# Loads of x0 and Wv in one queue on ACT, and half chunks of the output in three 64-row visits

## Chip, cores, metric

One core of a Trainium2 chip. The metric is the device time of one execution in microseconds (us), as the median of the runs in the fast state. "Span" is the length of the profiled execution, some 1.6 to 2.2 us less than the time. Ratios are the mean time of one kernel's fast runs over the mean of the other's fast runs of the same rounds, so not quite the ratio of the medians quoted beside them. The experiments ran on different chips. Kernels are compared only within the same rounds. Landings, waits and starts come from one profiled execution of each kernel.

## The reference, cut to what matters

```python
g = sigmoid((x * gate_w).sum(-1))                     # x: 2048 x 448
qkv = x @ wqkv                                        # 16 heads of 28
pq, pk = q @ w_phi, k @ w_phi                         # per head
phi = concat(softmax(p), softmax(-p))
kv, z = phi_k^T v, sum(phi_k)
a = (phi_q kv / (phi_q z + 1e-6)) @ wo
b = gelu(x @ w1 + b1) @ w2 + b2                       # 448 -> 1792 -> 448
out = g * a + (1 - g) * b
```

The kernel makes b and a in one PSUM tile per 128 rows of x: fourteen matmuls with w2 ("dense"), then those with wo. The quotient phi_q kv / den is made per tile in a "num" block (`nm`, `den`, `o_tok`) and transposed by a DMA into `oT`.

## The kernel before

The start. `gate` and the constants are left out; `...` marks cuts.

```python
nc.scalar.dma_start(x0, x[0:512, :] ...)                       # 448 KB
nc.sync.dma_start(gate[0:1, :], gate_w[None, :])
for c, eng in ((0, nc.sync), (1, nc.scalar), (2, nc.sync)):    # Wv, 112 KB each
    eng.dma_start(WvG[:, c, 0:D], A_wqkv[c * P:(c + 1) * P, 2 * D:3 * D])
nc.scalar.dma_start(WvG[64:P, 3, 0:D], A_wqkv[384:448, 2 * D:3 * D])
nc.scalar.dma_start(wphi[:, 0:3, :], ...)                      # 384 rows of 56 bytes
...
load_wT(WkT, D)            # DMA transposes of the key and query weights, on SP
load_wT(WqT, 0)
load_x(1)                  # DMA transposes of rows of x, on SP
...
dummies(7)                 # PE: keeps the array busy until x0 is there
turn_x0(0, xp[0])          # PE: 8 transposes, then a copy to xT
turn_gate()                # PE: gate's column; ACT casts it into column 448 of each WvG part
turn_x0(1, xp[1])
fill_bd()
v_pair(0, on_act=True)     # PE: V of tiles 0..3, needs all four parts of WvG
v_pair(1)
prep(WkT, ...)             # PE: first weight product (w_ps), needs WkT, then WqT
prep(WqT, ...)
```

The output. Four closing matmuls with wo (the fourth holds 64 rows of wo and b2) for tiles 0 to 3, three and a 64-row one for the others:

```python
for t in range(4):
    dense_out(y[:, 0:D], t, full, True, (6, 7) if t == 2 else ())   # num 6, 7 in its middle
    ...                                                              # num blocks, attn_out(..., NC4)
for g in range(4, NT, 4):
    ...
    y_ends(group[0:2], g)          # two pairs of 64-row matmuls open four tiles
    y_ends(group[2:4], g + 2)
    for t in range(g, g + 4):
        ...                        # dense_out, num blocks, attn_out(..., 3)
```

Ahead of it, while PE works on the 28 hidden units: `if n == 8: nc.sync.dma_start(w2_sb[:], ...)`, 1568 KB. It can't come sooner in one piece, since w2_sb's space holds q tokens until the DMA transposes have read them.

The softmax here doesn't subtract the row's maximum and nothing guards it: scores larger than these inputs give would overflow.

## Time and profile before

| | before |
|---|---|
| time, median (range) of the first three runs | 149.19 us (149.19 to 149.71) |
| span | 147.7 us |
| PE busy | 97% |
| x0 landed | 3.99 us |
| Wv's four parts landed (in the order 0, 1, 2, 3) | 4.88, 4.34, 5.53, 5.30 us |
| first V matmul / first weight product | 5.87 / 9.16 us |
| first num block to the start of the last matmul | 57.70 us |

Landings and starts are read from the trace's records; a landing is the time at which the semaphore of a DMA is full.

### The profile page before, as it was taken

What the parts mean: (1) busy time and instruction counts of PE and PEld (TensorE: products, weight loads), DVE (VectorE), ACT (ScalarE), POOL (GpSimd) and SP (SyncE); (2) the same over time, 40 slices, a digit from 0 to 9 for tenths busy, and PEclk for the clock granted to TensorE, in tenths of its full rate; (3) what the DMA queues carried; (4) which work ended last, traced back from release to release, by engine and by line L of the source; (5) the groups of instructions that cost most, each with busy time, mean ns of one, the idle gap of its engine ahead of it and who ended that gap; (6) DMA issues with size and microseconds to landing.
All of it is one profiled execution on the core that took longest, in us unless ns stands there. A gap on an engine that the chain in (4) does not pass through costs nothing.

```text
span 147.7 us, 3133 instructions
## 1 busy us (share of the span) xinstructions
PE 143.8 (97%) x1302; PEld 75.0 (51%) x1302; DVE 85.0 (58%) x134; ACT 75.3 (51%) x91; POOL 68.7 (47%) x50
## 2 busy tenths in 40 slices
PE   7999999999999999999999999999999999999992
PEld 2674545555544954444444455654555455545561
DVE  3443799999999899999200037760287237611112
ACT  1655999988899337777776760113211201221100
POOL 7999999999977999919940000000000000000000
PEclk9999999999999999999999999999999999999999
DMA  4999999999800099991999913394134103410111
GB/s 147 245 226 176 148 196 221 218 217 217 178 2 2 11 161 146 193 189 26 144 172 172 346 64 71 72 87 123 62 71 107 62 31 89 104 47 31 56 37 31
DMA packets 44962, 18.08 MB, mean 122 GB/s; under 512 B 36754, under 2 KB 44948, under 8 KB 44948
## 3 DMA queue, kind: packets, MB, share of 16 engines
q1 hardware_dynamic: 43732, 17.22, 59.2%
q10 hardware_dynamic: 1152, 0.65, 1.6%
q8 instruction: 10, 0.16, 0.5%
q14 instruction: 4, 0.03, 0.1%
q0 software_dynamic: 64, 0.01, 0.0%
HBM read 6.34 MB, written 1.84 MB: 55 GB/s over the span
## 4 chain that ended last, share of the span: by engine, by line
PE 97%; DVE 0%; issue 0%
PE y L520 29%; PE hp L467 29%; PE pq L348 7%; PE y L532 7%; PE v_ps L332 4%; PE pk L340 4%; PE pk L233 3%; PE nm L480 3%; PE acc L355 3%; PE v_ps L214 2%; PE warm_ps L386 2%; PE v_ps L233 2%; PE w_ps L264 1%; PE xp L369 1%; PE y L526 1%; PE pk L220 1%
## 5 line engine op out<-in xcount | busy, mean ns | idle before, releaser
L520 PE MATMUL y<-w_sb,gel 128*128 128x448 bf16 (+2 forms) x238 | 45.4, 342 | 0.0
L467 PE MATMUL hp<-xT,w_sb 64*128 64x512 bf16 x196 | 42.6, 376 | 0.0
L467 PE MATMUL hp<-xS,w_sb 64*128 64x512 bf16 x196 | 42.6, 376 | 0.0
L472 ACT ACTIVATE gel<-hp,b1T 128x1024 bf16<-128x1024 f32 x28 | 30.8, 1110 | 13.2 <-PE hp L467 13.2
L520 PEld LDWEIGHTS <-gel 128*128 128x128 bf16 x238 | 22.2, 98 | 19.8 <-issue 0.9
L467 PEld LDWEIGHTS <-w_sb 64*128 64x128 bf16 x392 | 18.9, 94 | 23.1
L308 POOL TENSOR_TENSOR phik<-phik,rec 128x1792 bf16<-128x1792 bf16 (+1 forms) x8 | 24.9, 3127 | 1.3 <-DVE rec L305 1.3
L546 ACT ACTIVATE b2u<-b_sb,ungate 128x448 f32<-128x448 bf16 x12 | 7.9, 666 | 28.7 <-DVE res L538 28.7
L484 DVE TENSOR_SCALAR den<-nm,einv 128x16 f32<-128x16 f32 x16 | 3.7, 229 | 29.5 <-PE nm L480 29.4
L538 DVE SCALAR_TENSOR_TENSOR res<-y,ungate,b2u 128x448 bf16<-128x448 f32 (+2 forms) x13 | 8.4, 648 | 17.1 <-PE y L532 17.1
L303 DVE TENSOR_REDUCE sums<-phik 128x64 f32<-128x1792 bf16 x8 | 16.0, 1999 | 3.2 <-ACT phik L294 3.2
L308 POOL TENSOR_TENSOR oT<-oT,rec 128x1792 bf16<-128x1792 bf16 x4 | 12.7, 3213 | 1.1 <-DVE rec L305 1.1
L532 PE MATMUL y<-wo_sb,oT 128*128 128x448 bf16 (+2 forms) x55 | 12.4, 342 | 0.0
L348 PE MATMUL pq<-Wpq,xT 64*128 64x448 bf16 x56 | 11.5, 349 | 0.0
L348 PE MATMUL pq<-WqS,xS 64*128 64x448 bf16 x56 | 11.4, 349 | 0.0
L308 POOL TENSOR_TENSOR w_sb<-w_sb,rec 128x1792 bf16<-128x1792 bf16 x3 | 9.6, 3213 | 3.0 <-DVE rec L305 3.0
L487 DVE TENSOR_TENSOR o_tok<-nm,den 128x448 bf16<-128x448 f32 x16 | 10.0, 624 | 0.6
L305 DVE RECIPROCAL rec<-sums 128x64 f32<-128x64 f32 x16 | 8.8, 553 | 1.9 <-DVE sums L303 0.5
L202 DVE CAST vaug<-v_ps 128x896 bf16<-128x896 f32 x7 | 7.5, 1072 | 3.0 <-PE v_ps L214 2.5
L536 ACT ACTIVATE res<-y,ungate 128x448 bf16<-128x448 f32 x4 | 2.5, 634 | 12.7 <-PE y L532 12.7
L293 ACT ACTIVATE phik<-pk 128x896 bf16<-128x896 f32 x8 | 7.6, 947 | 1.5 <-PE pk L222 1.5
L303 DVE TENSOR_REDUCE sums<-oT 128x64 f32<-128x1792 bf16 x4 | 7.9, 1973 | 0.0
(116 smaller groups left out, 180.6 us busy)
## 6 DMA issues: line engine op xcount, KB each, us to landing
w_sb<-in_B_w_dram SPq DMA_DIRECT2D x4, 784.0 KB, 11.5
out_dram<-res SPq DMA_DIRECT2D x15, 112.0 KB, 1.8
w_sb<-in_B_w_dram SPq DMA_DIRECT2D x1, 1568.0 KB, 7.3
xS<-xT SPq DMA_DIRECT2D x2, 256.0 KB, 4.0
EqT<-in_A_x_dram ACTq DMA_DIRECT2D x1, 448.0 KB, 3.2
xS<-xT SPq DMA_DIRECT2D x2, 192.0 KB, 3.9
wo_sb<-in_A_wo_dram SPq DMA_DIRECT2D x1, 336.0 KB, 16.9
oT<-o_tok SPq DMA_TRANSPOSE x16, 2.4
```

Of the source, the lines that this page charges most:

```text
L293: nc.scalar.activation(out=dst[:, :, :, 0, 0:PW], in_=src, func=ACT.Exp)
L303: nc.vector.reduce_sum(out=sums[:], in_=ph, axis=AX.X)
L305: nc.vector.reciprocal(out=rec[:], in_=sums[:])
L308: eng.tensor_tensor(out=ph[:, lo:hi], in0=ph[:, lo:hi], in1=rec[:, lo:hi, :, None].to_broadcast([P, hi - lo, 2, DH]), op=ALU.mult)
L348: nc.tensor.matmul(pq[:, i, 0:D], lhsT=x_half(i, k, h)[:, r * P:(r + 1) * P], rhs=w_half(Wpq, WqS, i, k), start=(k == 0), stop=(k == NK - 1))
L467: nc.tensor.matmul(hp[:, i, :], lhsT=w1_sb[i * HP:(i + 1) * HP, k, j * P:(j + 1) * P], rhs=x_half(i, k, h), start=(k == 0), stop=(k == NK ...
L472: nc.scalar.activation(out=gel[h][:, j, :], in_=hp[:].rearrange("p a b -> p (a b)"), func=ACT.Gelu_apprx_tanh, bias=b1T[:, j:j + 1])
L487: nc.vector.tensor_tensor(out=o_tok[:, t % 4, 0:D].rearrange("p (x h d) -> p x h d", x=NPR, h=2), in0=nmv[:, :, 0:PW].rearrange("p x (h d) ...
L520: nc.tensor.matmul(y, lhsT=gel[t // 8][:, j, (t % 8) * P:(t % 8 + 1) * P], rhs=w2_sb[:, j, cols], start=(opens and j == 0), stop=False)
L532: nc.tensor.matmul(y, lhsT=oT[:, c, tok], rhs=wo_sb[:, c, cols], start=False, stop=(c == chunks - 1))
L538: nc.vector.scalar_tensor_tensor(out=res[:, cols], in0=y, scalar=ungate[:, t:t + 1], in1=b2u[t][:, cols], op0=ALU.mult, op1=ALU.add)
L546: nc.scalar.activation(out=b2u[t][:], in_=b2_sb[:], func=ACT.Copy, scale=ungate[:, t:t + 1])
```

## The change

Its intent: x0, which PE waits for, gets through first, with all of Wv behind it in one queue, and the small load of w_phi goes to the otherwise idle SP; in the output, tiles 0 to 3 too use 64-row matmuls for their half chunk, and all sixteen are gathered in three visits.

```diff
-    for c, eng in ((0, nc.sync), (1, nc.scalar), (2, nc.sync)):
+    for c, eng in ((0, nc.scalar), (1, nc.scalar), (2, nc.scalar)):
         eng.dma_start(WvG[:, c, 0:D], A_wqkv[c * P:(c + 1) * P, 2 * D:3 * D])
     nc.scalar.dma_start(WvG[64:P, 3, 0:D], A_wqkv[384:448, 2 * D:3 * D])
-    nc.scalar.dma_start(wphi[:, 0:3, :], ...)
+    nc.sync.dma_start(wphi[:, 0:3, :], ...)
 ...
-    nc.sync.dma_start(wo_sb[:, 0:3, :], ...)          # and two small loads more
+    nc.sync.dma_start(wo_sb[:], ...)
 ...
-        if t % 2 and t > 3:
+        if t % 2:
             nc.vector.tensor_copy(out=o_tok[:, t % 4, D:512], in_=o_tok[:, t % 4, D - HP:D])
 ...
+    def visit(closing, opening):                      # 64-row matmuls, then DVE finishes `closing`
+        ...
+    ahead = {0: (2, 3), 1: (4, 5), 2: (6, 7), 3: (8,), 4: (9,), 5: (10, 11),
+             8: (12,), 9: (13,), 10: (14,), 11: (15,)}  # num blocks behind the dense part of a tile
+    ...
+        if t == 3:
+            visit((0, 1, 2, 3), (4, 5))
+        elif t == 7:
+            visit((6, 7), (8, 9, 10, 11))
+        elif t == 13:
+            visit((12, 13), (14, 15))
```

Also dropped: one memset on DVE, one on POOL. Tiles 0 to 3 are now finished by DVE instead of ACT.

More of the change, by code (lines that the diff above doesn't have):

```diff
@@ L77 @@
     w2_sb = consts.tile([P, NJ, D], BF16, name="w2_sb")
-    wo_sb = consts.tile([P, NC4, D], BF16, name="wo_sb")
+    wo_sb = consts.tile([P, 3, D], BF16, name="wo_sb")
     EqT = consts.tile([P, NPR, S], BF16, name="EqT")
@@ L127 @@
     nc.vector.memset(WvG[0:64, 3, :], 0.0)
-    nc.vector.memset(wo_sb[64:P, 3, :], 0.0)
     nc.vector.memset(Wpk[0:64, 3, :], 0.0)
@@ L133 @@
     nc.sync.dma_start(gate[0:1, :], gate_w[None, :])
-    for c, eng in ((0, nc.sync), (1, nc.scalar), (2, nc.sync)):
+    for c, eng in ((0, nc.scalar), (1, nc.scalar), (2, nc.scalar)):
         eng.dma_start(WvG[:, c, 0:D], A_wqkv[c * P:(c + 1) * P, 2 * D:3 * D])
     nc.scalar.dma_start(WvG[64:P, 3, 0:D], A_wqkv[384:448, 2 * D:3 * D])
-    nc.scalar.dma_start(wphi[:, 0:3, :], wphi_rows[0:384, :].rearrange("(c p) b -> p c b", p=P))
+    nc.sync.dma_start(wphi[:, 0:3, :], wphi_rows[0:384, :].rearrange("(c p) b -> p c b", p=P))
     def load_x(b, part=None):
@@ L186 @@
     nc.gpsimd.memset(phq3[:].rearrange("p i x s w -> p (i x s) w")[:, :, PW:HP], 0.0)
-    nc.gpsimd.memset(o_tok[:, :, D:D + 1], 1.0)
-    nc.gpsimd.memset(o_tok[:, :, D + 1:512], 0.0)
+    nc.gpsimd.memset(o_tok[:, :, D:512], 0.0)
     def fill_bd():
@@ L424 @@
                               B_w1[:, f].rearrange("(k p) f -> p k f", p=HP))
-    nc.sync.dma_start(wo_sb[:, 0:3, :], A_wo[0:384, :].rearrange("(c p) n -> p c n", p=P))
-    nc.sync.dma_start(wo_sb[0:64, 3, :], A_wo[384:448, :])
-    nc.sync.dma_start(wo_sb[64:65, 3, :], B_b2[None, :])
+    nc.sync.dma_start(wo_sb[:], A_wo[0:384, :].rearrange("(c p) n -> p c n", p=P))
     for i in range(2):
@@ L512, with dense_out @@
     ps2 = ctx.enter_context(tc.tile_pool(name="ps2", bufs=2, space=PSUM, reuse_waits="tile"))
-    def dense_out(y, t, cols, opens, mid=()):
+    def dense_out(y, t, cols, opens):
         for j in range(NJ):
-            if j == NJ // 2:
-                for n in mid:
-                    num_tile(n)
             nc.tensor.matmul(y, lhsT=gel[t // 8][:, j, (t % 8) * P:(t % 8 + 1) * P],
                              rhs=w2_sb[:, j, cols], start=(opens and j == 0), stop=False)
-    def y_ends(ys, t):
-        for i in range(2):
-            for y, cols in ys[i]:
-                nc.tensor.matmul(y, lhsT=oT[i * HP:(i + 1) * HP, 3, (t + i) * P:(t + i + 1) * P],
-                                 rhs=wo3[i * HP:(i + 1) * HP, cols], start=True, stop=False)
@@ L529, in attn_out @@
-    def attn_out(y, t, cols, chunks):
-        tok = slice(t * P, (t + 1) * P)
-        for c in range(chunks):
-            nc.tensor.matmul(y, lhsT=oT[:, c, tok], rhs=wo_sb[:, c, cols],
-                             start=False, stop=(c == chunks - 1))
-        res = work.tile([P, D], BF16, name="res", bufs=3)
-        if chunks == NC4:
-            nc.scalar.activation(out=res[:, cols], in_=y, func=ACT.Copy, scale=ungate[:, t:t + 1])
-        else:
-            nc.vector.scalar_tensor_tensor(out=res[:, cols], in0=y, scalar=ungate[:, t:t + 1],
-                                           in1=b2u[t][:, cols], op0=ALU.mult, op1=ALU.add)
-        nc.sync.dma_start(out2[tok, cols], res[:, cols])
+    def attn_out(y, t, cols, closes):
+        for c in range(3):
+            nc.tensor.matmul(y, lhsT=oT[:, c, t * P:(t + 1) * P], rhs=wo_sb[:, c, cols],
+                             start=False, stop=(closes and c == 2))
@@ new lines, in y_end, with finish @@
+    def y_end(y, t, cols, opens):
+        i = t % 2
+        nc.tensor.matmul(y, lhsT=oT[i * HP:(i + 1) * HP, 3, t * P:(t + 1) * P],
+                         rhs=wo3[i * HP:(i + 1) * HP, cols], start=opens, stop=not opens)
+    def finish(y, t, cols):
+        res = work.tile([P, D], BF16, name="res", bufs=3)
+        nc.vector.scalar_tensor_tensor(out=res[:, cols], in0=y, scalar=ungate[:, t:t + 1],
+                                       in1=b2u[t][:, cols], op0=ALU.mult, op1=ALU.add)
+        nc.sync.dma_start(out2[t * P:(t + 1) * P, cols], res[:, cols])
@@ L542, with y_tile @@
     b2u = {}
     def b2_tile(t):
-        b2u[t] = work.tile([P, D], F32, name="b2u", bufs=2)
+        b2u[t] = work.tile([P, D], F32, name="b2u", bufs=3)
         nc.scalar.activation(out=b2u[t][:], in_=b2_sb[:], func=ACT.Copy, scale=ungate[:, t:t + 1])
-    def y_tile():
-        return ps2.tile([P, 512], F32, name="y", tag="y", bufs=6)
-    full = slice(0, D)
-    parts = [slice(0, 336), slice(336, D)]
-    y = y_tile()
+    ys = {}
+    def y_tile(t):
+        parts = (slice(0, 336), slice(336, D)) if t == NT - 1 else (slice(0, D),)
+        ys[t] = [(ps2.tile([P, 512], F32, name="y", tag="y", bufs=6)[:, 0:c.stop - c.start], c)
+                 for c in parts]
@@ L554 @@
+    def visit(closing, opening):
+        for t in opening:
+            y_tile(t)
+        for tiles, opens in ((closing, False), (opening, True)):
+            for t in tiles:
+                for y, cols in ys[t]:
+                    y_end(y, t, cols, opens)
+        for t in closing:
+            b2_tile(t)
+            finish(ys[t][0][0], t, ys[t][0][1])
+    y_tile(0)
     num_tile(0)
     num_tile(1)
-    wait = []
-    for t in range(4):
-        y = y_tile() if t else y
-        dense_out(y[:, 0:D], t, full, True, (6, 7) if t == 2 else ())
-        wait.append((y[:, 0:D], t, full, NC4))
-        for n in ([2, 3], [4, 5], [], [])[t]:
-            num_tile(n)
-        while len(wait) > (1 if t < 3 else 0):
-            attn_out(*wait.pop(0))
@@ L565 @@
-    for g in range(4, NT, 4):
-        group = []
-        for t in range(g, g + 4):
-            group.append([(y_tile()[:, 0:c.stop - c.start], c)
-                          for c in (parts if t == NT - 1 else [full])])
-        y_ends(group[0:2], g)
-        y_ends(group[2:4], g + 2)
-        for t in range(g, g + 4):
-            b2_tile(t)
-            for y, cols in group[t - g]:
-                dense_out(y, t, cols, False)
-                if t - g < 2 and g + 4 < NT:
-                    for n in (2 * t - g + 4, 2 * t - g + 5):
-                        num_tile(n)
-                attn_out(y, t, cols, 3)
+    ahead = {0: (2, 3), 1: (4, 5), 2: (6, 7), 3: (8,), 4: (9,), 5: (10, 11),
+             8: (12,), 9: (13,), 10: (14,), 11: (15,)}
@@ new lines @@
+    closing = (0, 1, 2, 3, 6, 7, 12, 13)
+    for t in range(NT):
+        if t not in ys:
+            y_tile(t)
+        for y, cols in ys[t]:
+            dense_out(y, t, cols, t in closing)
+            for n in ahead.get(t, ()):
+                num_tile(n)
+            if t in (1, 2, 3):
+                attn_out(ys[t - 1][0][0], t - 1, slice(0, D), False)
+            if t in (0, 1, 2):
+                continue
+            attn_out(y, t, cols, t not in closing)
+            if t not in closing:
+                if cols.start == 0:
+                    b2_tile(t)
+                finish(y, t, cols)
+        if t == 3:
[4 more added lines that the diff above has]
+            visit((12, 13), (14, 15))
```

## The prediction

> **What bounds the kernel now.** I read, in this order, the page's first two parts, the chain that ended last, the timeline of the first 10 us, and the timelines of the output stage.
>
> ```profile
> PE 143.8 (97%) x1302; PEld 75.0 (51%) x1302; DVE 85.0 (58%) x134; ACT 75.3 (51%) x91; POOL 68.7 (47%) x50
> ...
> PE   7999999999999999999999999999999999999992
> ...
> PE 97%; DVE 0%; issue 0%
> ```
>
> TensorE is on the path for 97% of the span of 147.7 us, and no slice between the first and the last is below nine tenths. A busy PE could still hide waits, since its ends are modelled, so I took the records of consecutive matmuls and looked at the distance between their starts. From 6.5 us to 144 us almost every start follows the one before by the columns over 2.4 GHz plus 2 to 3 ns (0.189 us for 448 columns). Beyond that I found only these: about 0.1 us at every change between 128-row and 64-row matmuls, 0.058 us at 22.08, and 0.086 us at 95.98. So PE is bound by the number of matmuls: what a change takes from PE's own list, or from its start, is saved one to one. What it takes from any other engine is worth nothing.
>
> The start is the first part that the change touches:
>
> ```profile
> 2.75 1.49 PE L386 MATMUL warm_ps<-w_sb 128*128 128x512 bf16 x3
> 4.04 0.30 PE L369 MATMUL xp<-ident,EqT 128*128 128x128 bf16 x1
> ...
> 4.04 0.78 PEld L369 LDWEIGHTS <-EqT 128*128 128x128 bf16 x8 [0.71 <-DMA EqT<-in_A_x_dram]
> ...
> 5.12 0.69 DVE L202 COPY xT<-xp 128x1024 bf16<-128x1024 bf16 x1 [2.51 <-PE xp L369]
> 5.21 0.29 ACT L380 CAST WvG<-g_ps 128x1 bf16<-128x1 f32 x3 [0.66 <-PE g_ps L377]
> ...
> 5.87 3.45 PE L214 MATMUL v_ps<-WvG,xT 128*128 128x449 bf16 x16
> ```
>
> The reader is to see two things. PEld waited 0.71 us for x0, which landed at 3.99; that looks like a load on the path. But PE itself was not idle: seven dummy matmuls of 512 columns start every 0.427 us from 1.06, the last at 3.60, so they hold PE until 3.60 + 0.427 = 4.03. x0's transposes begin at 4.04. The load cost some 0.01 us. Then the V matmuls begin when the copy of xT is done (5.12 + 0.69 = 5.81), not when Wv comes.
>
> The output stage is the second part:
>
> ```profile
> 100.94 1.68 PE L532 MATMUL y<-wo_sb,oT 128*128 128x448 bf16 x8
> 102.54 0.55 PE L526 MATMUL y<-wo,oT 64*128 64x448 bf16 x4
> 103.03 2.82 PE L520 MATMUL y<-w_sb,gel 128*128 128x448 bf16 x14
> ...
> 95.67 0.69 PE L480 MATMUL nm<-KV,EqT 128*128 128x58 bf16 x16
> 96.21 0.35 PE L520 MATMUL y<-w_sb,gel 128*128 128x448 bf16 x1
> ```
>
> The first four tiles of rows use four output matmuls each (eight here for tiles 2 and 3), the fourth with only 65 useful rows. The other twelve use three, and a 64-row one that runs beside its partner in a visit (four records in 0.55 us, two pairs).
>
> **What the Trainium skill says.** First, "TensorEngine Tiling (Array Packing)", Key Properties: a change of tiling mode drains TensorE. The trace agrees: from the last 128-row start to the first 64-row start of the visit at 116.91 it is 0.285 us, and back 0.282 us, against 0.187 us of streaming; so a change costs about 0.1 us. This is why half chunks are gathered into few visits. Second, "TensorE: Matmul & The Clock Gate", Part 3, The mechanism: matmuls in different row groups run together, their starts about 4 ns apart. The trace agrees: 116.907 and 116.910, and the next pair 0.199 us later. Third, "DMA: Bandwidth & Descriptors", Issuing engines are not separate DMA queues: loads issued from SP and ACT run on the same 16 engines and interleave. The trace agrees: between 3.5 and 4.0 us packets of both queues ended (117 KB of ACT's, 56 KB of SP's). So one queue for x0 and Wv can let x0 through ahead of Wv, but does not make their sum shorter. Fourth, the Clock Gate page, Part 1, says that a cold array runs at half rate until some 3.4 us of activity; the dummies' 0.427 us (512 columns at 1.2 GHz) and the 0.189 us after 6.5 us agree.
>
> **The change part by part.**
>
> *The queues at the start.* x0 shares the DMA engines no longer with two Wv loads of SP, but only with the small loads and, from about 4 us, the first weight transpose, which SP issues some 0.45 us earlier. From the packets ACT's queue moved 187 KB in the half microsecond from 3.0, nearly alone. With that rate x0's 459 KB, which began to land near 1.9 us, are done by an estimated 3.5 to 3.8 instead of 3.99. The dummies are not shortened, so PE gains 4.04 - 4.03 = 0.01 us. The Wv parts come later. In the kernel before they landed at 4.34, 4.88, 5.30 and 5.53. After, four loads (401 KB) follow x0 in one queue and the last two share with transposes. ACT issues a DMA in 0.44 to 0.59 us, so the fourth part is issued near 3.0 and lands at an estimated 5.3 to 6.0. It is needed by the fourth V matmul, which started at 6.67. So it fits, with 0.6 us or more to spare. ACT issues five DMAs here as before it issued four: its issues end near 3.55 instead of 3.01, the table load (1.28 us) ends near 4.85 instead of 4.33, the dummy activation (0.20) near 5.05, and the gate's casts can start at 5.17, when their matmuls are done. It fits by 0.1 us, and if it did not, the casts have another half microsecond before the first V matmul. Sum: -0.01 us.
>
> *Small pieces off PE.* One memset of wo_sb (0.24 us of DVE at 2.04), one of o_tok (0.11 us of POOL), two DMA issues on SP: all beside other work, 0. The copy of 64 columns in o_tok is now made for tiles 1 and 3 too (2 x 0.18 us of DVE): DVE idles 0.83 us before each of the next den operations, so 0.
>
> *The output matmuls.* Before: 4 x 18 + 12 x 17 = 276 full ones; after: 16 x 17 = 272. Four less at 0.189 us: -0.76 us. The 64-row pairs rise from 6 to 8 (the visits go from 2, 2, 2 pairs to 3, 3, 2): two more at 0.20 us: +0.40 us. The visits stay three, so the changes of mode stay six: 0. Sum: -0.36 us.
>
> *The order of the num blocks.* Before, tiles 6 and 7 were put in the middle of tile 2's dense product, 2.5 us after the pair before; their PSUM buffer was not yet read by DVE, which is the 0.086 us at 95.98 (0.69 us instead of 0.62 for sixteen). After, they come behind the whole product, 1.3 us later: -0.09 us. Later pairs are split into single blocks; the matmuls are the same and start 29 ns apart, so 0.
>
> *Finishing of tiles 0 to 3* moves from ACT (0.63 us each) to DVE (0.68 us each, with b2u of 0.67 us on ACT), four in a burst after the first visit: an estimated 2.7 us, or 3.3 with a wait for the third result buffer. PE next needs DVE for the num blocks two tiles later, some 6 us after. And y's six banks: four closing tiles and two opened ones are exactly six; tile 6 takes tile 0's bank two tiles (6.4 us) after the visit. So 0.
>
> Total: -0.01 - 0.36 - 0.09 = -0.46 us. 149.19 - 0.46 = 148.73 us, or 148.7.
>
> **The rivals.** *The load was the bound:* if the 0.71 us of PEld's wait were time on the path, an earlier x0 would give up to 0.4 us more and 148.3. Against it stand the dummies' starts. For it: unprofiled runs may see x0 later than this one. *Wv becomes the bound:* with everything behind x0 and the transposes beside it, the third or fourth part could land after 6.5 and hold PE by 0.2 to 0.8 us: 149.0 to 149.5. For it: the transposes' packets filled all engines from 5.5 on, and nothing orders the two queues. Against it: 0.6 us of slack. *The banks or DVE become the bound* in the output stage, because four tiles stay open until the visit: each wait for a bank would cost up to 0.7 us, perhaps twice, and 149.5 or more. Against it: the spacing of 6.4 us. *More pairs eat it up:* if the eight pairs did not run side by side, four more 64-row matmuls would replace four 128-row ones and only 0.1 us would be left: 149.1.
>
> **Range and chances.** The sum of what I count is 0.3%, and the three runs before already spread over 0.52 us. Rivals that lose are worth up to 0.8 us and I give them a quarter together; the one that gains 0.4 us I give a tenth. That makes 148.2 to 149.4. Two per cent are 3.0 us; nothing that I found is of that size: faster 0.01, same 0.98, slower 0.01.
>
> **What would show it.** The dummies still end at 4.03 and the transposes start there, though x0 lands by 3.8. V's first matmul starts at 5.85 within 0.05. The last Wv part lands before 6.3, with no gap between the first V matmuls beyond that of the clock. The matmuls on y fall by four full ones, the 64-row records rise from 13 to 17, in visits of 3, 3 and 2 pairs with 0.20 us per pair. No start on PE in the output stage lags by over 0.05 us other than at six changes of mode. The distance from the first num block to the end shrinks by 0.45 us. The prediction is wrong if the gain is found ahead of 9 us instead, or if PE waits for WvG, for a bank of y or for nm.

## More of the kernel before

What bounds the kernel is read step by step in the prediction. Three lines of its timeline were not used there and turn out to matter (start, duration, engine; "SPq" is SP issuing a DMA):

```profile
1.69 0.85 SPq L135 DMA_DIRECT2D WvG<-in_A_wqkv_dram  x2
...
2.58 2.31 SPq L147 DMA_TRANSPOSE WkT<-in_A_wqkv_dram  x1
...
9.16 1.09 PE L264 MATMUL w_ps<-w_sb,WkT 128*128 128x140 bf16 x16
```

SP issues two parts of Wv and only then, at 2.58 us, the first DMA transpose. Those two parts stand in front of the transposes in SP's own queue. The last line is the first weight product.

## The result

| | before | after |
|---|---|---|
| time, median (range) of six runs each | 149.38 us (149.19 to 150.56) | 154.56 us (153.77 to 155.33) |
| ratio of the fast runs, 95% interval | | 1.0335 (1.0287 to 1.0383) |
| span | 147.7 us | 153.2 us |
| x0 landed | 3.99 us | 4.06 us |
| Wv's parts 0, 1, 2, 3 landed | 4.88, 4.34, 5.53, 5.30 | 4.37, 6.14, 8.17, 9.56 |
| first V matmul | 5.87 us | 6.44 us |
| first weight product | 9.16 us | 15.00 us |
| from there to the first num block | 77.76 us | 77.85 us |
| first num block to the last matmul's start | 57.70 us | 57.24 us |
| from there to the end | 3.04 us | 3.16 us |

The kernel is 3.35% slower, where 0.3% faster was predicted. The last four rows say where: 5.84 us are lost before the first weight product, and the output stage gains 0.46. (5.84 + 0.09 - 0.46 + 0.12 = 5.59; the spans differ by 5.58.)

The page of the kernel after, with the row of the granted clock, and the chain:

```profile
PE 145.7 (95%) x1302; PEld 75.5 (49%) x1302; DVE 87.8 (57%) x139; ACT 75.2 (49%) x91; POOL 68.6 (45%) x49
...
PE   7649999999999999999999999999999999999992
...
PEclk9955999999999999999999999999999999999999
...
PE 92%; DMA 4%; ACTq 1%; DVE 0%; issue 0%; ACT 0%
```

PE's second and third slice fall to six and four tenths, the granted clock to five tenths in the third and fourth, and a DMA now stands in the chain for 4%. The timeline of the kernel after, at the start:

```profile
1.28 1.50 ACTq L134 DMA_DIRECT2D WvG<-in_A_wqkv_dram  x3
...
2.18 2.94 SPq L146 DMA_TRANSPOSE WkT<-in_A_wqkv_dram  x1
...
2.81 0.77 ACTq L135 DMA_DIRECT2D WvG<-in_A_wqkv_dram  x1
...
6.44 0.54 PE L212 MATMUL v_ps<-WvG,xT 128*128 128x449 bf16 x2 [0.75 <-ACT WvG L378]
...
8.21 0.10 PEld L212 LDWEIGHTS <-xT 128*128 128x128 bf16 x1 [1.68 <-DMA WvG<-in_A_wqkv_dram]
...
9.58 0.16 ACT L378 CAST WvG<-g_ps 128x1 bf16<-128x1 f32 x1 [3.13 <-DMA WvG<-in_A_wqkv_dram]
...
9.79 5.41 PE L212 MATMUL v_ps<-WvG,xT 128*128 128x449 bf16 x14 [2.81 <-ACT WvG L378]
...
15.00 1.22 PE L262 MATMUL w_ps<-w_sb,WkT 128*128 128x140 bf16 x16
```

Two V matmuls run at 6.44; the other fourteen wait until 9.79, behind a cast on ACT into WvG (9.58), which waits for a DMA of WvG. By the landings this DMA is part 3 (9.56): the cast writes into part 2, and part 2, for which PEld waits at 8.21, had landed at 8.17. In run 12 too this cast comes at 9.33, just behind part 3 (9.31), though part 2 was there at 6.83. So Wv's last part set the start of the fourteen. Then they take 5.41 us, where the kernel before needed 3.45 for all sixteen: their starts are 0.374 us apart, the half rate. PE had been idle, and its clock was down. So the 5.84 us are two things. The third V matmul starts 3.32 us later than before (9.79 against 6.47). From there to the first weight product it takes 5.21 us instead of 2.69: another 2.52.

The waits of the kernel after (who waited for whom; us in total, times, longest):

```profile
ACT WvG L378 <- DMA WvG<-in_A_wqkv_dram: 4.2, 2, 3.1
...
PEld L212 <- DMA WvG<-in_A_wqkv_dram: 3.6, 3, 1.7
```

The kernel before has no wait for WvG's DMA at all. Why the parts came late, the DMA views of the same two microseconds show, 4.5 to 6.5. Kernel before:

```profile
DMA packets 2216, 0.54 MB, mean 270 GB/s; under 512 B 2129, under 2 KB 2216, under 8 KB 2216
...
q1 hardware_dynamic: 1820, 0.51, 110.9%
q10 hardware_dynamic: 396, 0.03, 14.0%
```

Kernel after:

```profile
DMA packets 1122, 0.38 MB, mean 189 GB/s; under 512 B 961, under 2 KB 1122, under 8 KB 1122
...
q1 hardware_dynamic: 937, 0.23, 68.9%
q10 hardware_dynamic: 184, 0.14, 41.6%
```

q1 is SP's queue, q10 ACT's; the columns are packets, MB, and the time that packets took as a share of sixteen engines. Before, ACT's queue is nearly through (0.03 MB) and SP's queue, with the rest of its own Wv and then the transposes, runs nearly alone. After, ACT's queue still holds 0.14 MB of Wv that moves in this time, beside the transposes, and both together move less than before: 189 GB/s instead of 270.

The output stage of the kernel after, at its first visit:

```profile
106.63 1.30 PE L518 MATMUL y<-wo_sb,oT 128*128 128x448 bf16 x6
...
107.86 0.74 PE L523 MATMUL y<-wo,oT 64*128 64x448 bf16 x6
...
108.53 1.69 PE L513 MATMUL y<-w_sb,gel 128*128 128x448 bf16 x8
```

Six closing matmuls with wo instead of eight, and three pairs of 64-row matmuls instead of two; from the visit's first matmul to the next dense one it is 0.67 us, against 0.49 before. That is as predicted.

### The profile page after: what moved, and what is told of

Same layout as the page of the kernel before. It is cut to its first block, busy times and chain, and to the rows that moved or that the text cites. A ratio compares the mean times of both kernels' runs of the same rounds, so it can differ in the third digit from the quotient of the medians.

```text
span 153.2 us, 3136 instructions
## 1 busy us (share of the span) xinstructions
PE 145.7 (95%) x1302; PEld 75.5 (49%) x1302; DVE 87.8 (57%) x139; ACT 75.2 (49%) x91; POOL 68.6 (45%) x49
## 4 chain that ended last, share of the span: by engine, by line
PE 92%; DMA 4%; ACTq 1%; DVE 0%; issue 0%; ACT 0%
PE y L513 28%; PE hp L463 28%; PE pq L346 7%; PE y L518 6%; DMA WvG<-in_A_wqkv_dram 4%; PE v_ps L212 4%; PE v_ps L330 3%; PE pk L338 3%; PE pk L231 3%; PE acc L353 2%; PE nm L476 2%; PE v_ps L231 2%; PE w_ps L262 1%; PE y L523 1%; ACTq L134 1%; PE pk L218 1%
## 5 line engine op out<-in xcount | busy, mean ns | idle before, releaser
L536 ACT ACTIVATE b2u<-b_sb,ungate 128x448 f32<-128x448 bf16 x16 | 10.2, 666 | 40.8 <-DVE res L528 40.8
L528 DVE SCALAR_TENSOR_TENSOR res<-y,ungate,b2u 128x448 bf16<-128x448 f32 (+2 forms) x17 | 10.8, 653 | 15.4 <-PE y L523 10.1
L518 PE MATMUL y<-wo_sb,oT 128*128 128x448 bf16 (+2 forms) x51 | 11.7, 341 | 0.0
L212 PE MATMUL v_ps<-WvG,xT 128*128 128x449 bf16 x16 | 6.0, 550 | 3.6 <-ACT WvG L378 3.6
```

The lines of the kernel that those rows point to most:

```text
L212: nc.tensor.matmul(v_ps[:, i, 0:D + 1], lhsT=xT[:, c, t * P:(t + 1) * P], rhs=WvG[:, c, :], start=(c == 0), stop=(c == NC4 - 1))
L518: nc.tensor.matmul(y, lhsT=oT[:, c, t * P:(t + 1) * P], rhs=wo_sb[:, c, cols], start=False, stop=(closes and c == 2))
L528: nc.vector.scalar_tensor_tensor(out=res[:, cols], in0=y, scalar=ungate[:, t:t + 1], in1=b2u[t][:, cols], op0=ALU.mult, op1=ALU.add)
L536: nc.scalar.activation(out=b2u[t][:], in_=b2_sb[:], func=ACT.Copy, scale=ungate[:, t:t + 1])
```

## The experiments

Theory after the result: DMA transposes of SP that are in flight beside ACT's queue starve that queue, and the change took away what had held them back: two parts of Wv ahead of them in SP's queue. Rivals: one queue is too slow for x0 and four parts; the 384 small packets of w_phi on SP disturb; the output stage or the memory layout has a part in it.

**1. Only the output stage changed.** The changed kernel with the loads of the start as before:

```diff
-    for c, eng in ((0, nc.scalar), (1, nc.scalar), (2, nc.scalar)):
+    for c, eng in ((0, nc.sync), (1, nc.scalar), (2, nc.sync)):
 ...
-    nc.sync.dma_start(wphi[:, 0:3, :], ...)
+    nc.scalar.dma_start(wphi[:, 0:3, :], ...)
```

> The changed kernel with the loads of the start put back as they were before; only the output stage (and the dropped memset and two loads) changed. Theory (starved Wv): the loss is all at the start, so this is 0.46 us faster than before, about 148.9 against 149.4; first num block to the last matmul start 57.24 us as in the changed kernel, against 57.70 before; first matmul of the weight products at 9.16. Rival (the output stage costs time too): 149.4 or more.

Measured: 150.74 us (149.58 to 151.06, six runs) against 149.65 (149.47 to 150.77); ratio 1.0037 (0.9994 to 1.0080). The loss of 3.35% is gone, so it does sit in the queues. But the gain of 0.46 did not show either, and the profiled run says why (starts, durations, and what ended the idle time before them):

```profile
10.29 1.10 PE L262 MATMUL w_ps<-w_sb,WqT 128*128 128x140 bf16 x16 [0.55 <-DMA WqT<-in_A_wqkv_dram]
...
88.75 2.43 PE L513 MATMUL y<-w_sb,gel 128*128 128x448 bf16 x12 [1.02 <-DMA w_sb<-in_B_w_dram]
```

Here V was done 0.5 us sooner than in the profile of before (first weight product at 8.66), and PE then waited for the second transposed weight, WqT, which landed at 10.25. And the first output matmul waited for w2, which landed at 88.62. In the profile of before these two landed at 9.98 and 86.31, against 10.09 and 87.39 when PE wanted them: they were within 0.1 and 1.1 us of being the bound. My reading of "PE alone is the path" had overlooked both. The output stage without that wait is 58.42 - 1.19 = 57.23 us here (1.19 is the gap between the starts around it, beyond the matmul's own time), as predicted.

**2. Only the queues changed**, in the kernel before (the two lines above the other way).

> The kernel before with only the four changed issue queues of the start. Theory: the whole loss is here: 155.0 (about 5.6 us over before), Wv's third and fourth part landing at 8 to 10 us, first weight product near 15.0. Rival (memory layout, the smaller tile or the output stage have a part in the late loads): landings and time in between, 150 to 153.

Measured: 154.79 us (154.41 to 155.15); ratio 1.0325 (1.0279 to 1.0370). Wv's parts landed at 4.44, 6.39, 8.85 and 10.40, the first weight product started at 14.96. So these two lines are, within the noise, the whole loss.

**3. The transposes wait for Wv.** The changed kernel, with one small copy on SP that reads all of Wv, ahead of the transposes:

```diff
+    landed = consts.tile([P, NC4, 16], BF16, name="landed")
+    nc.sync.dma_start(landed[64:80], WvG[64:80, :, 0:16])
     load_wT(WkT, D)
```

> The changed kernel, but ahead of its first DMA transpose SP issues one small copy that reads all four parts of Wv, so that the transposes start only when Wv has landed. Theory (transposes of the other queue starve Wv): Wv's four parts land by 5.6 us though all are in one queue behind x0, V matmuls start at 5.9 and run to 9.2; then the late weight transposes cost PE some 1 us, so 149.5 to 151. Rival (one queue is too slow for x0 and four parts): landings at 6.1, 8.2 and 9.6 as in the changed kernel and 154 or more.

Measured: 154.81 us (154.28 to 155.52). PE's timeline:

```profile
6.00 3.46 PE L214 MATMUL v_ps<-WvG,xT 128*128 128x449 bf16 x16
11.97 1.10 PE L264 MATMUL w_ps<-w_sb,WkT 128*128 128x140 bf16 x16 [2.51 <-DMA WkT<-in_A_wqkv_dram]
```

Wv, all in ACT's queue behind x0, landed at 4.47, 5.57, 5.87 and 6.04, and the sixteen V matmuls ran from 6.00 in 3.46 us without a wait. So one queue is fast enough, and the rival falls. The time was no better, because the copy could be issued only at 6.13 and the transposes behind it at 6.96, and WkT landed at 11.93: PE waited 2.5 us there, and the clock fell again. I had put that cost at some 1 us. The transposes are as much in a hurry as Wv is.

**4. PE kept warm in the wait.** The changed kernel with 16 more dummies behind x0's transposes:

```diff
+    w_first = dummies(7)      # was: dummies(7)
 ...
     turn_x0(1, xp[1])
+    dummies(16, w_first)      # into the same PSUM tile
```

> The changed kernel with 16 more dummy matmuls of 512 columns after x0's transposes, in the time in which PE waits for Wv. Theory: of the 5.8 us some 3.2 us are the wait itself and 2.6 us the clock that is cold again, fourteen V matmuls at 0.374 instead of 0.189 us. With dummies the landings stay at 6.1, 8.2 and 9.6, the V matmuls run at 0.189, and the time falls by 2.3 to 2.8 us, to about 152.0. Rival (the half rate comes from the operands' arrival or the DMA traffic, not from PE's idleness): V matmuls still at 0.374 and 154.5.

Measured: 154.05 us (153.42 to 154.95), 0.5 us below the changed kernel's median; ratio to before 1.0261. It was run at another time. The mechanism held and the size in the time did not. The V matmuls ran at 0.189 us, but in the profiled run Wv landed later still (7.30, 10.40, 10.86), and the first output matmul waited 0.82 us for a result of ACT, which no run without the extra dummies showed; it is a cost of my edit. The trace gives the clock's share more cleanly: from the landing of Wv's last part to the first weight product it is 5.44 us in the changed kernel (9.56 to 15.00) and 3.01 here (10.86 to 13.87). Run 11 repeats it.

**5. All of Wv in one queue on SP**, ahead of the transposes, and w_phi on ACT behind x0.

> The changed kernel with all four parts of Wv in one queue again, but on SP, ahead of the transposes; x0 alone with the small load of w_phi on ACT. Theory (a load in the other queue is starved once SP's transposes run; one behind another in the same queue is not): all of Wv lands by 5.9 us and the V matmuls run from 5.7 to 9.1 without a wait; the first weight transpose is issued some 0.4 us later than in the kernel before and may hold the weight products by up to 0.5 us; 149.0 to 150.8. Rival (all Wv in one queue is what is slow): a part of Wv after 6.5, a cold clock, 152 or more.

Measured: 150.90 us (150.21 to 151.73), ratio 1.0091 (1.0020 to 1.0163). Wv landed at 4.75, 5.41, 6.51 and 6.79: the last two were 0.6 to 0.9 us later than expected, and PE waited 0.48 us for them. But no starvation: one queue behind another costs 1% (within the 2% below which the verdict is "same"), two queues against each other 3%. The order of before is still the better one.

**6. Only part 2 of Wv moved to ACT**; part 0 and w_phi as before.

> The changed kernel with part 0 of Wv and w_phi back where they were, so only part 2 has moved from SP to ACT. Theory (what is still in ACT's queue when the transposes' packets begin, near 4.3 us, is starved, and the later in the queue the worse): parts 0 and 1 land by 4.9, part 2 near 5.5 to 6.5, part 3 at 6 to 8, and w_phi, which is last, at 7 to 9; loss between none and 3.5 us: 149.5 to 153. Rival (only the number of bytes in a queue counts): all of Wv by 5.6 and no loss.

Measured: 153.04 us (one run, state unknown). Parts 0 and 1 landed by 5.13, part 2 at 5.65, part 3 at 6.75, w_phi, last in ACT's queue, at 8.16. V ran from 5.96 with one wait of 0.61 us; then DVE, which needs w_phi, held the weight products for 0.67 and 1.24 us, and w2, which landed at 90.89, the first output matmul for 1.0 us. What stands last in ACT's queue is late.

**7. w_phi back to the end of ACT's queue**, all else as changed.

> The changed kernel with the small load of w_phi put back from SP to the end of ACT's queue. Rival (the 384 small packets of w_phi on SP are what slows Wv): parts 2 and 3 land by 6 us, 149 to 150. Theory (the transposes do): they start 0.4 us earlier, so parts 2 and 3 land at 8 to 11 us and w_phi still later, 154.5 to 156.

Measured: 156.82 us (one run, state unknown). SP's first transpose was issued at 1.69 us, and Wv landed at 6.05, 10.52, 11.65 and 11.90, w_phi at 12.28. So the small packets are not the cause; without them the transposes come 0.5 us sooner and the harm is larger. The same two microseconds, 4.5 to 6.5:

```profile
DMA packets 411, 0.14 MB, mean 69 GB/s; under 512 B 361, under 2 KB 411, under 8 KB 411
```

Both queues had work, and together they moved 69 GB/s. This is not a fair sharing of a full engine: for much of the time little moved at all.

**8. A plain load beside Wv.** The changed kernel with 448 KB more of x on SP ahead of the transposes, into a place that is overwritten later.

> The changed kernel with one more plain load on SP ahead of the transposes, 448 KB like x0, into a place that is overwritten later. It puts plain packets beside Wv where the transposes' were, and the transposes behind them. Theory (it is the transposes' packets, not just any traffic of SP, that starve ACT's queue): Wv's parts share the engines with the plain load and land by 6.5 us, the last at 5.8 to 6.5, two to three us sooner than in the changed kernel although as many bytes lie beside them; the weight products are then late by 1 to 3 us because of the late transposes; 150.5 to 154. Rival (any two full queues share so badly): parts 2 and 3 at 8 us or later.

Measured: 154.00 us (one run, state unknown); Wv at 4.55, 6.96, 8.38 and 8.56. The expectation (6.5 or sooner) missed. The run mixed two things: the first transpose was issued at 4.33, with Wv and the plain load still on their way. Run 13 mends that.

**9 and 10. w2 in three parts**, for the changed output stage and for the kernel before, since w2's landing had come up as a second bound:

```diff
-        if n == 8:
-            nc.sync.dma_start(w2_sb[:], ...)
+        if n in (5, 6, 8):
+            lo, hi = {5: (0, 4), 6: (4, 9), 8: (9, NJ)}[n]
+            nc.sync.dma_start(w2_sb[:, lo:hi, :], B_w2[lo * P:hi * P, :] ...)
```

> The run with only the output stage changed (150.7, between 149.6 and 151.1; its profile showed 1.02 us of PE waiting for w2 before the first output matmul), with w2 loaded in three parts as the space comes free instead of one load at the end. Theory (the output stage does save 0.46 us, and a late w2 had taken it back and more): w2's last part lands by 84 us, no wait at the first output matmul, 148.7 to 149.2, all runs within 0.4 us. Rival (something else in the output stage costs): 149.5 to 151 again.

> The kernel before with w2 loaded in the same three parts. Theory (the runs of the kernel before at 150.6 to 150.8 are those in which w2 was late, the others had none of it to lose): 149.2 to 149.7 and none above 150.2; so 0.0 to 0.3 us less than the kernel before in the mean. Rival (the slower runs have another cause): runs at 150.7 stay.

Measured: changed output 149.60 us (149.17 to 149.72), before 149.84 (149.66 to 150.03), the unaltered kernel before 150.47 (149.27 to 151.25, ten fast runs; an eleventh, at 152.87, was slow). The ratios to the latter are 0.9958 (0.9914 to 1.0002) and 0.9977 (0.9933 to 1.0020). The last part of w2 landed at 88.5 and 88.6, not by 84 as expected, but the matmuls that need it come later than the first nine of the first tile; neither profile has a wait there. Both kernels lost the runs above 150.1, of which the kernel before has some in every larger set (150.4 to 151.3). That fits a late w2 as their cause; no run of the kernel before at that time was profiled, so it isn't shown. Between the two the output stage gains 0.24 us in the medians; in the traces, first num block to last matmul, it is 57.70 and 57.24, 0.46. In the rest of them other waits differ (WqT held PE for 0.79 us in the one and 0.57 in the other). This version is the fastest that I ran, but it isn't clear of the noise.

**11 and 12. The changed kernel with w2 in three parts**, with and without the 16 dummies.

> The changed kernel with the 16 more dummies in PE's wait and with w2 in three parts, so that a late w2 can't take the gain back. Theory (2.6 us of the loss are the cold clock): V matmuls at 0.189 us and a time 2.0 to 2.8 us below the run of the changed kernel with w2 in three parts alone, in this same call. Rival (the clock costs little because the weights are late anyway): within 0.7 us of it.

> The changed kernel with w2 in three parts alone. Theory (its loss is at the start, w2 is not in it): 153.8 to 155.3, as the changed kernel itself, with Wv's last part at 9 to 11 us. Rival (w2 late is a part of the loss): below 153.5.

Measured: 153.39 us (152.93 to 153.66) with, 153.91 (152.48 to 154.02, three fast runs; a fourth, at 154.99, was slow) without: 0.5 us, within the spread, and not 2.0 to 2.8. Against the kernel before both are unclear at the limit of 2% (ratios 1.0205 and 1.0219). w2 has no large part in the loss, though one fast run lies below the 153.5 that was set for the rival. The timeline with the dummies:

```profile
6.10 3.62 PE L384 MATMUL warm_ps<-w_sb 128*128 128x512 bf16 x16
9.56 3.23 PE L212 MATMUL v_ps<-WvG,xT 128*128 128x449 bf16 x16
12.63 1.09 PE L262 MATMUL w_ps<-w_sb,WkT 128*128 128x140 bf16 x16
```

Wv's last part landed at 9.60, nearly as in the changed kernel (9.56), and the first weight product came at 12.63 instead of 15.00: 2.4 us of the loss there is the clock. That less of it shows in the time has two reasons in the traces: again 0.82 us of waiting at the first output matmul, and the profiled run without dummies lost less: Wv's last part landed at 9.31, and only from 10.07 to 13.07 do V's starts lie 0.374 us apart (in the changed kernel from 10.12 to the end), so the first weight product was at 13.89.

**13. A plain load beside Wv, and the transposes held back** until Wv has landed (runs 3 and 8 in one).

> The changed kernel with the transposes held back until Wv has landed (as in the third run) and in addition a plain load of 448 KB on SP beside Wv. It mends the eighth run, in which the first transpose was issued while Wv was still on its way. Theory A (transposes, by their issue or their packets, are what starves ACT's queue): Wv's parts, sharing the engines with plain packets only, land at 4.5, 5.5, 6.2 and 6.7 us or earlier. Theory B (any second full queue does it): the third and fourth part at 8 us or later. The time, 154 to 157, says nothing here, since the transposes are late.

Measured: Wv at 4.45, 6.75, 7.60 and 7.83; 156.40 us (one run, state unknown). This lies between the two theories. A second full queue of plain packets delays Wv's last part by 1.8 us against run 3 (6.04), the transposes by 3.5 (9.56; 3.3 to 4.8 over the five profiles in which they were issued at 2.16 to 2.18). What differs is the sum. From 4.5 to 6.5:

```profile
DMA packets 622, 0.51 MB, mean 256 GB/s; under 512 B 51, under 2 KB 622, under 8 KB 622
```

Two plain queues moved 256 GB/s together; Wv and transposes 189 in the changed kernel and 69 in run 7. So two full queues share, which costs the one that is in a hurry, and with transposes in the second they also lose throughput.

**14. The transposes issued later**, by two tiny loads ahead of them on SP.

> The changed kernel with two tiny loads (2 KB each) on SP ahead of the transposes, where the two parts of Wv had been issued before, so that the first transpose is issued at 2.9 to 3.1 us instead of 2.18, a little later than in the kernel before (2.58). If the earlier issue of the transposes is most of the harm: the last part of Wv at 6.5 us or sooner and 150 to 151.5. If it is that all of Wv stands in the other queue behind x0: last part at 7.5 us or later and 152 to 154.5.

Measured: 150.44 us, the kernel before 150.45 beside it (one run each, state unknown). The transposes were not issued near 3.0: SP waited until 4.15, by the trace for a load of x, and ACT's fourth part of Wv went out at 4.13 instead of 2.81, so the edit moved more than I meant. Parts 0 to 2, issued at the same times as in the changed kernel, landed at 4.43, 5.55 and 6.24 instead of 4.37, 6.14 and 8.17, part 3 at 6.69 (6.5 or sooner had been expected), V ran from 6.27 to 9.69, and the whole loss was gone, though all of Wv stood in ACT's queue.

Taken by the time at which the first transpose was issued, with all of Wv on ACT and no plain load beside it, the third part's landing goes one way: 1.69 us, 11.65; 2.18 us, 8.17; 4.15 us, 6.24; 6.96 us, 5.87. But the spread at one issue time is wide: in the five profiles with 2.16 to 2.18 (the changed kernel, runs 2, 4, 11 and 12) it landed between 6.83 and 10.40, the last part between 9.31 and 10.86. The trend holds for the last part too (11.90 at 1.69, 6.69 at 4.15, 6.04 at 6.96); a single landing says little.

## Why the prediction was wrong, step by step

**The queues at the start: wrong, and this is the step that failed.** The sum said that the fourth part of Wv "lands at an estimated 5.3 to 6.0" and the whole step is worth -0.01 us. It landed at 9.56 and the step cost +5.84. I had counted bytes and issue times, and assumed that ACT's queue keeps its share beside the transposes. I saw the transposes come 0.45 us sooner, and saw them fill the engines, and put no cost on their meeting Wv. Runs 1 and 2 show that the step is the whole loss; 3, 7 and 14 that it depends on when the transposes begin; 3 and 5 that one queue is not the fault. What the change took away was the two parts of Wv ahead of the transposes in SP's queue, which had kept them back until ACT's queue was nearly empty.

**The casts of the gate "start at 5.17": wrong.** They waited for Wv: those of parts 0 and 1 for part 1's landing (6.22), those of parts 2 and 3 for part 3's (9.58), and ACT's copy of xT stood behind them (9.95 instead of 6.08).

**x0 by "3.5 to 3.8": wrong, and without effect.** It landed at 4.06, and between 4.04 and 4.32 in the runs, with or without Wv on SP. That the dummies hide it was right but for 0.07 us: the transposes start at 4.11 instead of 4.04.

**The second cost, the cold clock, was missing.** I knew the half rate from the dummies and did not ask what an idle PE would do to it. By the traces it is 2.4 to 2.5 us of the 5.84. The wait need not be long for it: in run 8 PE waited 0.89 and 0.64 us ahead of V's first and third matmul, and from the fourth on the starts lay 0.374 us apart too.

**The output stage: right.** Four matmuls less, two pairs more, and num 6 and 7 out of the middle: -0.36 - 0.09. The distance to the last matmul's start fell from 57.70 to 57.24 us (to the end of the span, as the prediction had put it, by 0.34, since the end took 3.16 instead of 3.04), the 64-row records are 17, the gap at num 7 is gone, and the only late starts are the six changes of mode, 0.1 us each. DVE's burst and the six banks cost nothing. In the time of the whole kernel the gain isn't clear of the noise (runs 1 and 9).

**"Saved one to one": only in part.** WqT and w2 land close to when PE wants them, and take back what is saved ahead of them (run 1).

**The rivals.** "Wv becomes the bound" was the right one, at 0.2 to 0.8 us; it was seven times the upper end. So the range was too narrow at the upper end, and 0.01 for slower by over 2% was far too low. "Against it: 0.6 us of slack" was slack against my own estimate, not one that a trace had shown.

**What stays open:** why loads and transposes in two queues move so little. In run 4 no packet of either queue started between 5.6 and 6.2 us, with Wv's parts 1 to 3 and both weight transposes still to land (the DMA view of that stretch):

```profile
DMA packets 0, 0.00 MB, mean 0 GB/s; under 512 B 0, under 2 KB 0, under 8 KB 0
```

That speaks against mere sharing, but no run shows what blocks them. It may sit in the issuing and not in the packets: SP took 1.86 us to issue the second weight transpose in the kernel before, 3.58 after, 5.56 in run 4 and 6.36 in run 7. No run separates the two. Nor does one separate the earlier transposes from the added bytes in ACT's queue; run 14 was to do it and moved both.

## What to carry to other kernels

A load that stands ahead of another in a queue is also a brake on it: before moving it to "its own" queue, ask what will then start sooner and beside whom. Keep plain loads that PE is waiting for clear of DMA transposes of the other queue, by putting them ahead of the transposes in the same queue or by issuing the transposes when they are nearly through, but not much later: held back until 6.96 us they cost as much (run 3). And where a late input leaves PE idle at the start, count the wait and, beside it, the half rate of the matmuls that follow.

## What the Trainium skill lacked or had wrong

- "DMA: Bandwidth & Descriptors", Rules for kernel authors, says, in a row on results that get corrupted, that a transpose next to ordinary DMAs needs nothing. For correct results no run here speaks against it; for time it did not hold here. With transposes of SP beside them, Wv's loads landed up to 6.7 us after their issue (9.3 in run 7) instead of 3.1 to 3.5, and both queues together moved 189 GB/s (69 in run 7) where transposes nearly alone or two plain queues moved 270 and 256.
- The same page, Issuing engines are not separate DMA queues, says that starting DMAs on several engines only saves the sequencer's time for starting them. Here it decided the order in which transposes and loads met, and two changed lines cost 3.25% (run 2).
